# Linear attention and a highway layer on one core: the query turns of two batches moved to DMA, and batch 2's and 3's buffers rearranged

## The chip, the core and the metric

One core of a Trainium2 chip runs the whole program in one launch. The metric is the device time in microseconds, start of the program to its end. The kernel before was run 7 times: median 132.7 us, 132.04 to 135.15. One execution was taken with the hardware profiler. Its engines are TensorE (PE; PEld is its weight load), VectorE (DVE), ScalarE (ACT), GpSimd (POOL) and SyncE (SP), which issues the DMA transfers.

## What is computed

```python
# q, k, v: 8 batches, 8 heads, 576 positions, 64 columns, float32
q_s = exp(q) / sum(exp(q), over the 64 columns)
k_s = exp(k) / sum(exp(k), over the 576 positions)
kv  = einsum('bhsd,bhse->bhde', k_s, v)            # 64x64 per head
x   = einsum('bhsd,bhde->bhse', q_s, kv)           # 576x64 per head
x   = x.transpose(0, 2, 1, 3).reshape(4608, 512)   # 8 heads side by side
H   = maximum(x @ w_h, 0)                          # 512x512
T   = sigmoid(x @ w_t + b_t)
out = T * H + (1 - T) * x                          # float32
```

## The kernel before, in words

**Attention, batch by batch.** A batch's q, k and v lie in SBUF with two heads on the 128 partitions (64 positions of each), and four head pairs (c) times 9 blocks of positions (n) times 64 columns along a row. For batch b: `exp_half` (line 176) takes the exponential of half the heads of q or k on ACT, float32 in and 16 bits out (eq, ek). `q_sums` (225) sums eq over columns on DVE, `q_recip` (246) inverts the sums, and `q_scale_p` (257) multiplies eq by them on GpSimd, blocks 0 to 3 and then the rest. `cast_v` (186) turns v to 16 bits on GpSimd, with a column of ones. `kv_half` (203) accumulates ek's product with v in a two-bank PSUM tile (psk); the ones column gives k's sums, and `kv_norm` (216) divides by them on DVE into kvn.

The x matmuls need eq with its columns on the partitions. `q_trans` (261) does this turn: group 0 is blocks 0 to 3, group 1 blocks 4 to 7, group 2 block 8. For each block it issues two TensorE matmuls against the identity (`ptrans`, 67) into one PSUM bank (pq), and DVE copies the bank to qsT (line 277): 18 turns and 3 copies a batch. The bank is that of the pool ps_1, which holds one tile ("single"), unless a home is given.

`x_pair` (310), for a = 0 and 1, multiplies kvn by qsT for blocks 0 to 7 of half the heads: four matmuls of 512 columns into two banks (px), which ACT ("A") or DVE ("V") copies to xT. Block 8 is done for 64 columns at a time, inside x_pair (left=True) or by `x_left` (296), and goes to x9.

**The highway layer, chunk by chunk.** A chunk is the 512 tokens of a batch (chunks 8 and 9 hold the x9 tokens), and each has four output blocks (ob). `gate` (357) multiplies w_t by xT into a bank (pt) and ACT takes tanh in place; `carry` (368) multiplies w_h (halved and less the identity) by xT into a bank (ph), which DVE folds into dd (line 383); `blend` (388) combines pt and dd to g on DVE (line 391); `add_x` (398) adds x on GpSimd for some blocks. `out_tile` (415) turns g (and x, where it was not added) back on TensorE, copies the result to SBUF, and after every fourth block SP issues a store of 1 MB.

**PSUM.** There are eight banks: four in a ring for pt and ph (ps_ht), two held together (ps_2, `two_banks`), and one each in ps_1 (`single`) and ps_nat (`nat_bank`). A new tile in a pool waits until the tile whose place it takes has been read.

**The order of the work** is written out by hand, and each engine runs its own instructions in that order. Lines 553 to 584 give the start as a list. Everything later has a due time in slots (`at`, line 482), and the sorted slots are issued one after another. Chunk c begins at slot 8c: gate ob at 8c + 2 ob, carry one slot later, blend two slots later. Batch b's attention is placed relative to p = 8 (b - 1) (lines 516 to 549): e0, e1 for the two exponentials of q, s0, s1 for the sums, sc for the scaling, and the triples tr, kv and x for the three turns, the kv halves and the x pairs. The loads of batches 4 to 7 (line 550) are issued on SP at slot 8 (b - 3), in the same queue as the stores.

Of the kernel before, what the change touches and what calls it, by code (L numbers as in the profile page):

```python
# [9 lines left out]
FP32 = mybir.dt.float32  # L10
FP16 = mybir.dt.float16
# [7 lines left out]
def kernel(  # L19
# [10 lines left out]
    nc = tc.nc  # L30
    B, H, S, D = q.shape
    P = 128
    PAD = 128
    N9 = S // 64
# [5 lines left out]
    def heads_view(t, b):  # L40
# [9 lines left out]
    eqp = pool("eqp", 2)  # L50
    small = pool("small", 2)
    qtp = pool("qtp", 2)
    xtp = pool("xtp", 3)
    gp = pool("gp", 2)
    mo = pool("mo", 3)
    ps_ht = pool("ps_ht", 4, space=PSUM)
# [6 lines left out]
    mm = lambda o, l, r, st, sp: nc.tensor.matmul(  # L63
        o, l, r, start=st, stop=sp, skip_group_check=True
    )
# [12 lines left out]
    kvn = [consts.tile([P, 2, 2, 64], FP16, name=f"kvn{i}") for i in range(2)]  # L78
# [80 lines left out]
    def two_banks(name, dt=FP32):  # L159
        return ps_2.tile([P, 2, 2048 // (4 if dt is FP32 else 2)], dt, tag="q2", name=name)  # L160

    single = lambda name: ps_1.tile([P, 512], FP32, tag="q1", name=name)
    nat_bank = lambda name, dt=FP32: ps_nat.tile(
        [P, 512 if dt is FP32 else 1024], dt, tag="nat", name=name
# [5 lines left out]
            mm(t, ident, wide, True, True)  # L170


    ek, eq, psk, qsT = {}, {}, {}, {}
    xT, gT = {}, {}

    def exp_half(b, which, a):
# [36 lines left out]
                        n == 0, n == N9 - 1,  # L213
                    )

    def kv_norm(b):
        rz = small.tile([P, 2, 2], FP32, tag="rz", name=f"rz_{b}")
        nc.vector.reciprocal(rz, psk[b][:, :, :, 64])
        nc.vector.tensor_mul(
            kvn[b % 2], psk[b][:, :, :, 0:64], rz.broadcast_to([P, 2, 2, 64])  # L220
        )

    qsum = {}
# [37 lines left out]
    def q_trans(b, g, home=None):  # L261
# [14 lines left out]
                )  # L276
        nc.vector.tensor_copy(qsT[b][:, :, n0:n1, :], t[:, :, 0:w, :])  # L277

    def x_mm(dst, b, a, c, x, n0, n1):
        r = slice(64 * c, 64 * c + 64)  # L280
        mm(
            dst[64 * x : 64 * x + 64], kvn[b % 2][r, x, a, :],
            qsT[b][r, 2 * a + x, n0:n1, :].rearrange("p n d -> p (n d)"), True, True,
        )


    def x9_mm(t, b, c):
# [4 lines left out]
    def x9_copy(b, t, c=slice(0, 2)):  # L292
        x9v = x9.rearrange("p (a c) b d -> p c a b d", c=2)
        nc.vector.tensor_copy(x9v[:, c, :, b, :], t)

    def x_left(b):
        for c in range(2):
            name = f"px_{b}_l{c}"
            t = single(name) if c == 0 else two_banks(name)[:, 0] if b == 1 else nat_bank(name)
            t = t[:, 0:128].rearrange("p (z a w) -> p z a w", z=1, a=2)  # L300
            for a in range(2):
                for x in range(2):
                    x_mm(t[:, 0, a, :], b, a, c, x, NM, N9)
            x9_copy(b, t, slice(c, c + 1))
# [2 lines left out]

    def x_pair(b, a, how, left=False, singles=False):  # L310
        g, b2 = b // 2, b % 2
        if a == 0 and b2 == 0:
            xT[g] = xtp.tile([P, 4, NM, 2, 64], FP16, tag="xT", name=f"xT_{g}")
        if left and a == 0:
            t9 = ps_1.tile([P, 512], FP32, tag="q1", name=f"px_{b}_l")
            x9t[b] = t9[:, 0:256].rearrange("p (c a w) -> p c a w", c=2, a=2)
        if singles:
            t = [
                ps_ht.tile([P, 512], FP32, tag="ht", name=f"px_{b}_{a}_{c}")
                for c in range(2)  # L320
            ]
        else:
            t2 = two_banks(f"px_{b}_{a}")
            t = [t2[:, c] for c in range(2)]
        if left and a == 0:
            x9_mm(x9t[b], b, 0)
        for c in range(2):
            for x in range(2):
                x_mm(t[c], b, a, c, x, 0, NM)
        if left and a == 1:  # L330
            x9_mm(x9t[b], b, 1)
        dst = xT[g][:, 2 * a : 2 * a + 2, :, b2, :]
        view = lambda t: t.rearrange("p (n d) -> p n d", d=64)
        copy = {"A": nc.scalar.copy, "V": nc.vector.tensor_copy}
        if len(how) == 1:
            copy[how](dst, t2.rearrange("p c (n d) -> p c n d", d=64))  # L336
        else:
            for c in range(2):
                copy[how[c]](dst[:, c], view(t[c]))  # L339
        if left and a == 1:  # L340
            x9_copy(b, x9t[b])
# [140 lines left out]
    def at(p, *fs):  # L482
        events.setdefault(p, []).extend(fs)

    E = lambda f, *a: (lambda: f(*a))

    for c in range(1, B + 2):
        for ob in range(4):
            p = 8 * c + 2 * ob
# [6 lines left out]
    for g in range(B // 2):  # L496
        p = 16 * (g + 1)
# [6 lines left out]
    p = 8 * B + 8  # L504
# [3 lines left out]

    at(8, E(cast_v_head, 2, 0, nc.gpsimd), E(q_scale_p, 2, 0, 4), E(q_scale_p, 2, 4, 8))
    at(8.2, E(x_left, 1))  # L510
    at(9, E(exp_half, 2, "k", 0))
    at(10, E(cast_v_head, 2, 1, nc.scalar), E(exp_half, 2, "k", 1))
    at(10.5, E(blend, 0, 3))
# [7 lines left out]
    for b in range(2, B):  # L521
        p = 8 * (b - 1)
        if b > 2:
            e0, e1, s0, s1, sc = {
                3: (-2.6, -1.6, -1.1, -0.1, 1),
                4: (-5.5, -4.5, -3.7, -2.7, -2.6),
            }.get(b, (-5, -4, -3.9, -2.9, -2.8))
            at(p + e0, E(exp_half, b, "q", 0))
            at(p + e1, E(exp_half, b, "q", 1))
            at(p + s0, E(q_sums, b, 0))  # L530
            at(p + s1, E(q_sums, b, 1), E(q_recip, b))
            at(p + sc, E(q_scale_p, b, 0, 4), E(q_scale_p, b, 4, N9))
            s = p + {3: 0, 4: 0}.get(b, -0.5)
            at(s, E(exp_half, b, "k", 0), E(cast_v, b, 0))
            at(s + 0.9, E(cast_v, b, 1))
            at(s + 1, E(exp_half, b, "k", 1))
        tr, kv, x = {
# [3 lines left out]
        }.get(b, ((2, 3, 4), (4, 4), (5, 6)))  # L541
        for i in range(3):
            at(p + tr[i], E(q_trans, b, i))
        at(p + kv[0], E(kv_half, b, 0))
        at(p + kv[1], E(kv_half, b, 1), E(kv_norm, b))
        at(p + x[0], E(x_pair, b, 0, "A", b > 2))
        at(p + x[1], E(x_pair, b, 1, "AV" if b == 2 else "A", b > 2, b == 2))
        if b == 2:
            at(p + 7.6, E(x_left, 2))
    for b in range(4, B):  # L550
        at(8 * (b - 3), *[E(load, b, w) for w in "qkv"])

    for f in [
        E(warm_up, 24),
        E(exp_half, 0, "q", 0), E(q_sums, 0, 0),
        E(exp_half, 0, "q", 1), E(q_sums, 0, 1),
        E(q_recip, 0), E(q_scale_v, 0, 0, 4), E(q_scale_v, 0, 4, N9),
        E(exp_half, 0, "k", 0), E(cast_v, 0, 0),
        E(exp_half, 0, "k", 1), E(cast_v, 0, 1),
        E(q_trans, 0, 0), E(q_trans, 0, 1, lambda: two_banks("pq_0_1", FP16)[:, 0]), E(warm_up, 2), E(q_trans, 0, 2, lambda: nat_bank("pq_0_2", FP16)),  # L560
        E(warm_up, 6),
        E(kv_half, 0, 0), E(gate_bias), E(warm_up, 2), E(kv_half, 0, 1), E(kv_norm, 0),
        *[E(cast_weight, "t", k_, (nc.vector, nc.gpsimd)[k_ % 2]) for k_ in range(4)],
        E(warm_up, 4),
        E(x_pair, 0, 0, "AA"), E(warm_up, 2), E(x_pair, 0, 1, "AV", False, True), E(warm_up, 1), E(x_left, 0),
        E(exp_half, 1, "q", 0), E(q_sums_tree, 1, 0),
        E(exp_half, 1, "q", 1), E(q_sums_tree, 1, 1), E(q_recip, 1),
        *[f for k_ in range(4) for f in (E(less_one, k_), E(cast_weight, "h", k_, nc.scalar, 0.5))],
        E(q_scale_p, 1, 0, 4), E(q_scale_p, 1, 4, 8),
        E(gate, 0, 0), E(gate, 0, 1), E(gate, 0, 2, lambda: two_banks("pt_0_2")[:, 0]), E(warm_mid, 5),  # L570
        E(carry, 0, 0), E(blend, 0, 0), E(carry, 0, 1), E(exp_half, 1, "k", 0),
        E(gate, 0, 3, lambda: nat_bank("pt_0_3")), E(blend, 0, 1), E(carry, 0, 2),
        E(q_trans, 1, 0), E(blend, 0, 2), E(carry_products, 0, 3),
        E(exp_half, 1, "k", 1),
        *[E(cast_v_head, 1, c, (nc.scalar, nc.gpsimd, nc.gpsimd, nc.scalar)[c]) for c in range(4)],
        E(q_scale_p, 1, 8, N9),
        *[E(load, 2, w) for w in "qk"], E(load, 2, "v", [nc.sync, nc.sync]),
        *[E(load, 3, w) for w in "qkv"],
        E(q_trans, 1, 1), E(kv_half, 1, 0), E(kv_half, 1, 1), E(kv_norm, 1),
        E(q_trans, 1, 2), E(carry_diff, 0, 3), E(exp_half, 2, "q", 0),  # L580
        E(x_pair, 1, 0, "AV"), E(x_pair, 1, 1, "AV", False, True),
        E(q_sums_tree, 2, 0), E(exp_half, 2, "q", 1), E(q_sums_tree, 2, 1), E(q_recip, 2),
    ]:
        f()
    for p in sorted(events):
# [32 lines left out]
```

The softmax here doesn't subtract the row's maximum and nothing guards it: scores larger than these inputs give would overflow.

## Time and profile before

| | |
|---|---|
| runs | 132.7 us median of 7, 132.04 to 135.15 |
| profiled execution | 132.04 us, of which the span is 130.2 us |
| granted TensorE clock, mean | 0.988 |
| TensorE busy, span slices 69 to 114 us | 10.97 of 11, 11.96 of 12, 10.97 of 11, 10.97 of 11 us |
| TensorE idle, 36 to 57 us | 4.25 us |
| loads to landing, median | 13.7 us (q), 13.2 us (k), 13.8 us (v); 1152 KB each |
| stores of 1 MB to landing, median | 5.2 us |

The span is what the profile covers, from the first instruction to the last. A profile row gives the source line, the engine, the operation, its output and inputs by name with their shape, how often it came, the busy time and the mean duration of one, and the idle time of the engine just before such instructions with what ended it. A row of the timeline has the start and the length first, and in brackets the idle time before it and who ended that. Busy matmuls overlap: the 219 ns of a small matmul are its latency, and eight of them in a row take 0.45 to 0.6 us. In the chain of waits each row is a piece of the path that ended last, with its start and its share of that path.

### The profile page before, as it was taken

What the parts mean: (1) busy time and instruction counts of PE and PEld (TensorE: products, weight loads), DVE (VectorE), ACT (ScalarE), POOL (GpSimd) and SP (SyncE); (2) the same over time, 40 slices, a digit from 0 to 9 for tenths busy, and PEclk for the clock granted to TensorE, in tenths of its full rate; (3) what the DMA queues carried; (4) which work ended last, traced back from release to release, by engine and by line L of the source; (5) the groups of instructions that cost most, each with busy time, mean ns of one, the idle gap of its engine ahead of it and who ended that gap; (6) DMA issues with size and microseconds to landing.
All of it is one profiled execution on the core that took longest, in us unless ns stands there. A gap on an engine that the chain in (4) does not pass through costs nothing.

```text
span 130.2 us, 3470 instructions
## 1 busy us (share of the span) xinstructions
PE 114.8 (88%) x1431; PEld 64.6 (50%) x1431; DVE 99.8 (77%) x183; ACT 92.3 (71%) x129; POOL 70.3 (54%) x64
## 2 busy tenths in 40 slices
PE   4999997984988798499989999999999999999940
PEld 1345442461435346255645664465556445688930
DVE  1397537796999997986899679988997656669960
ACT  3643159987898499287979988998994666576430
POOL 2004516880299999549835990799299704600000
PEclk9999999999999999999999999999999999999995
DMA  4999999999999999996999999992034007065874
GB/s 127 371 380 388 402 401 412 411 411 413 403 413 410 402 412 412 403 411 251 290 375 413 412 267 413 405 433 118 0 146 181 0 5 322 0 252 234 362 309 140
DMA packets 15847, 40.06 MB, mean 308 GB/s; under 512 B 724, under 2 KB 1240, under 8 KB 14808
## 3 DMA queue, kind: packets, MB, share of 16 engines
q1 hardware_dynamic: 15832, 39.85, 79.3%
q8 instruction: 11, 0.18, 0.5%
q14 instruction: 4, 0.03, 0.1%
HBM read 30.41 MB, written 9.44 MB: 306 GB/s over the span
## 4 chain that ended last, share of the span: by engine, by line
PE 47%; DMA 19%; DVE 14%; POOL 8%; SPq 3%; issue 2%; ACT 2%; DVEq 0%; POOLq 0%
DMA q<-in_q_dram 19%; PE pt L63 17%; PE ph L63 15%; PE nat L63 6%; POOL eq L259 3%; PE pq L68 3%; DVE dd L383 3%; POOL g L400 3%; DVE g L391 2%; PE px L63 2%; PE psk L63 2%; SPq L95 2%; DVE r L229 2%; POOL v L192 2%; DVE xT L339 1%
## 5 line engine op out<-in xcount | busy, mean ns | idle before, releaser
L259 POOL TENSOR_TENSOR eq<-eq,r 128x1024 f16<-128x1024 f16 (+2 forms) x16 | 29.7, 1875 | 14.9 <-DVE r L247 14.3
L63 PE MATMUL pt<-xT,w16t 128*128 128x512 f16 x128 | 33.7, 379 | 2.8 <-DVE dd L383 1.3
L63 PE MATMUL ph<-xT,w16h 128*128 128x512 f16 x128 | 33.3, 380 | 1.1 <-ACT w16h L115 0.7
L365 ACT ACTIVATE pt<-pt,bt 128x512 f32<-128x512 f32 (+1 forms) x40 | 24.7, 621 | 12.0 <-PE pt L63 11.2
L391 DVE SCALAR_TENSOR_TENSOR g<-pt,dd 128x512 f16<-128x512 f32 (+1 forms) x40 | 25.0, 628 | 3.1 <-DVE dd L383 0.5
L383 DVE SCALAR_TENSOR_TENSOR dd<-xT,ph 128x512 f16<-128x512 f16 x32 | 21.8, 682 | 6.7 <-PE ph L63 6.6
L400 POOL TENSOR_TENSOR g<-g,xT 128x512 f16<-128x512 f16 x18 | 20.5, 1152 | 7.6 <-DVE g L391 7.5
L63 PEld LDWEIGHTS <-w16t 128*128 128x128 f16 x160 | 14.6, 97 | 18.1 <-issue 5.6
L180 ACT ACTIVATE eq<-q 128x1152 f16<-128x1152 f32 x16 | 18.6, 1174 | 5.2 <-DMA q<-in_q_dram 5.2
L180 ACT ACTIVATE ek<-k 128x1152 f16<-128x1152 f32 x16 | 18.6, 1172 | 1.7 <-DMA k<-in_k_dram 1.7
L63 PEld LDWEIGHTS <-w16h 128*128 128x128 f16 x160 | 13.7, 98 | 11.3 <-ACT w16h L115 2.4
L229 DVE TENSOR_REDUCE r<-eq 128x18 f32<-128x1152 f16 x12 | 16.1, 1344 | 3.8 <-ACT eq L180 3.7
L192 POOL CAST v<-v 128x1152 f16<-128x1152 f32 x12 | 13.5, 1146 | 10.0 <-DMA v<-in_v_dram 10.0
L63 PE MATMUL nat<-ident,g 128*128 128x128 f16 x142 | 17.7, 219 | 0.5 <-DVE g L391 0.2
L63 PEld LDWEIGHTS <-g 128*128 128x128 f16 x144 | 13.7, 98 | 7.1 <-DVE g L391 1.4
L336 ACT CAST xT<-px 128x1024 f16<-128x1024 f32 x11 | 11.2, 1016 | 7.2 <-PE px L63 7.2
L440 ACT COPY o<-nat 128x512 f32<-128x512 f32 x26 | 15.6, 600 | 0.1
L63 PE MATMUL warm<-wide,ident 128*128 128x512 f16 x41 | 12.8, 462 | 1.8 <-DVE wide L152 1.8
L68 PE MATMUL pq<-ident,eq 128*128 128x128 f16 x144 | 12.0, 219 | 2.7 <-DVE qsT L277 2.1
L277 DVE COPY qsT<-pq 128x1024 f16<-128x1024 f16 (+1 forms) x24 | 13.2, 553 | 1.1 <-PE pq L68 0.6
L68 PEld LDWEIGHTS <-eq 128*128 128x128 f16 x144 | 9.3, 97 | 7.0 <-issue 3.3
L63 PE MATMUL nat<-ident,xT 128*128 128x128 f16 x56 | 9.7, 219 | 0.0
(52 smaller groups left out, 100.3 us busy)
## 6 DMA issues: line engine op xcount, KB each, us to landing
out_dram<-o SPq DMA_DIRECT2D x8, 1024.0 KB, 5.2
q<-in_q_dram SPq DMA_DIRECT2D x7, 1152.0 KB, 13.7
k<-in_k_dram SPq DMA_DIRECT2D x7, 1152.0 KB, 13.2
v<-in_v_dram SPq DMA_DIRECT2D x5, 1152.0 KB, 13.8
v<-in_v_dram SPq DMA_DIRECT2D x6, 576.0 KB, 11.8
q<-in_q_dram SPq DMA_DIRECT2D x2, 576.0 KB, 4.0
k<-in_k_dram SPq DMA_DIRECT2D x2, 576.0 KB, 7.0
w32t<-in_moe_w_t_dram SPq DMA_DIRECT2D x1, 1024.0 KB, 10.9
```

Of the source, the lines that this page charges most:

```text
L63: mm = lambda o, l, r, st, sp: nc.tensor.matmul(o, l, r, start=st, stop=sp, skip_group_check=True)
L68: nc.tensor.matmul(o, i, ident, is_transpose=True, start=True, stop=True, skip_group_check=True,)
L180: nc.scalar.activation(dst[b][:, :, 2 * a : 2 * a + 2, :], in32[which][b][:, 2 * a : 2 * a + 2].rearrange("p c n d -> p n c d"), AF.Exp,)
L192: (eng or nc.gpsimd).tensor_copy(o, i)
L229: nc.vector.reduce_sum(qsum[b][:, :, h], eq[b][:, :, h, :], axis=AX.X)
L259: nc.gpsimd.tensor_mul(e, e, r.broadcast_to(list(e.shape)))
L277: nc.vector.tensor_copy(qsT[b][:, :, n0:n1, :], t[:, :, 0:w, :])
L365: nc.scalar.activation(ps, ps, AF.Tanh, bias=bt2[:, ob : ob + 1], scale=0.5)
L383: nc.vector.scalar_tensor_tensor(dd, xv(ob), -0.5, ps, op0=ALU.mult, op1=ALU.max)
L391: nc.vector.scalar_tensor_tensor(gv(ob), th, 1.0, dd, op0=ALU.add, op1=ALU.mult)
L400: nc.gpsimd.tensor_add(gv(ob), gv(ob), xv(ob))
L440: nc.scalar.copy(o, flat(t))
```

## The change

Four things are rearranged, and the values computed stay the same.

1. Batches 6 and 7: `q_trans` is replaced by `q_turn`, which issues two transposing DMA transfers on SP (blocks 0 to 3, then 4 to 8) from eq to a tile qsD in SBUF; the x matmuls read it with a stride. The exponentials, sums and scaling of these batches come one slot earlier. The transfers are due at slot p - 2.05.
2. Batch 2: kv_norm is done for each half (a) by itself, the x pairs come earlier and use ps_nat and ps_1 as their banks, both pairs' copies go half by half (ACT and ACT, then ACT and DVE), and its `x_left` comes later.
3. Batch 1: the x pairs use banks of the ring (the last half one of the two-bank tile), and their copies come ahead of batch 2's first exponential.
4. Batches 2 and 3: the last turn (block 8) uses the two-bank tile instead of the single bank. The sums and the scaling of batch 4, and the sums of batch 5, come later.

```diff
+    ht_bank = lambda name: ps_ht.tile([P, 512], FP32, tag="ht", name=name)
+    one_of_two = lambda name: two_banks(name)[:, 0]
...
-    def kv_norm(b):
-        rz = small.tile([P, 2, 2], FP32, tag="rz", name=f"rz_{b}")
-        nc.vector.reciprocal(rz, psk[b][:, :, :, 64])
+    def kv_norm(b, a0=0, a1=2):
+        w = a1 - a0
+        rz = small.tile([P, 2, w], FP32, tag=f"rz{w}", name=f"rz_{b}_{a0}")
+        nc.vector.reciprocal(rz, psk[b][:, :, a0:a1, 64])
         nc.vector.tensor_mul(
-            kvn[b % 2], psk[b][:, :, :, 0:64], rz.broadcast_to([P, 2, 2, 64])
+            kvn[b % 2][:, :, a0:a1], psk[b][:, :, a0:a1, 0:64],
+            rz.broadcast_to([P, 2, w, 64]),
         )
...
+    turned = (6, 7)
+
+    def q_turn(b, n0, n1):
+        if n0 == 0:
+            qsD[b] = qtp.tile([P, 2 * N9, P], FP16, tag="qsT", name=f"qsD_{b}")
+            qsT[b] = qsD[b].rearrange("p (n a) (x k) -> p (a x) n k", a=2, x=2)
+        nc.sync.dma_start_transpose(
+            out=qsD[b][:, 2 * n0 : 2 * n1, :],
+            in_=eq[b][:, n0:n1].rearrange("p n c d -> p (n c d)"),
+        )
+
     def x_mm(dst, b, a, c, x, n0, n1):
         r = slice(64 * c, 64 * c + 64)
-        mm(
-            dst[64 * x : 64 * x + 64], kvn[b % 2][r, x, a, :],
-            qsT[b][r, 2 * a + x, n0:n1, :].rearrange("p n d -> p (n d)"), True, True,
-        )
+        rhs = qsT[b][r, 2 * a + x, n0:n1, :]
+        if b not in turned:
+            rhs = rhs.rearrange("p n d -> p (n d)")
+        elif n1 - n0 == 1:
+            rhs = rhs[:, 0]
+        else:
+            dst = dst.rearrange("p (n d) -> p n d", d=64)
+        mm(dst[64 * x : 64 * x + 64], kvn[b % 2][r, x, a, :], rhs, True, True)
...
-            t = single(name) if c == 0 else two_banks(name)[:, 0] if b == 1 else nat_bank(name)
+            t = single(name) if c == 0 else one_of_two(name) if b > 0 else nat_bank(name)
...
-    def x_pair(b, a, how, left=False, singles=False):
+    def x_pair(b, a, how, left=False, homes=None):
...
-        if singles:
-            t = [
-                ps_ht.tile([P, 512], FP32, tag="ht", name=f"px_{b}_{a}_{c}")
-                for c in range(2)
-            ]
+        if homes:
+            t = [home(f"px_{b}_{a}_{c}") for c, home in enumerate(homes)]
...
+    at(16.2, E(x_left, 2))
...
-                4: (-5.5, -4.5, -3.7, -2.7, -2.6),
+                4: (-5.5, -4.5, -2.8, -1.5, -1.4),
+                5: (-5, -4, -3.4, -2.7, -2.6),
+                6: (-6, -5, -4.9, -3.9, -3.8),
+                7: (-6, -5, -4.9, -3.9, -3.8),
             }.get(b, (-5, -4, -3.9, -2.9, -2.8))
...
-            2: ((5, 6, 6.9), (4, 6.2), (7, 7.5)),
-            3: ((3.5, 4.9, 5.1), (4, 4), (5.9, 6.9)),
+            2: ((5, 6, 7.1), (4, 6.2), (6.5, 7.2)),
+            3: ((3.5, 4.9, 4.95), (4, 4), (5.9, 6.9)),
             4: ((2, 3, 4), (4.5, 4.5), (5.9, 6.9)),
         }.get(b, ((2, 3, 4), (4, 4), (5, 6)))
-        for i in range(3):
-            at(p + tr[i], E(q_trans, b, i))
+        if b in turned:
+            at(p - 2.05, E(q_turn, b, 0, 4), E(q_turn, b, 4, N9))
+        else:
+            for i in range(3):
+                home = (lambda: two_banks("pq_t", FP16)[:, 0]) if b < 4 and i == 2 else None
+                at(p + tr[i], E(q_trans, b, i, home))
         at(p + kv[0], E(kv_half, b, 0))
-        at(p + kv[1], E(kv_half, b, 1), E(kv_norm, b))
-        at(p + x[0], E(x_pair, b, 0, "A", b > 2))
-        at(p + x[1], E(x_pair, b, 1, "AV" if b == 2 else "A", b > 2, b == 2))
         if b == 2:
-            at(p + 7.6, E(x_left, 2))
+            at(p + kv[0], E(kv_norm, b, 0, 1))
+            at(p + kv[1], E(kv_half, b, 1), E(kv_norm, b, 1, 2))
+        else:
+            at(p + kv[1], E(kv_half, b, 1), E(kv_norm, b))
+        homes = (nat_bank, single) if b == 2 else None
+        at(p + x[0], E(x_pair, b, 0, "AA" if b == 2 else "A", b > 2, homes))
+        at(p + x[1], E(x_pair, b, 1, "AV" if b == 2 else "A", b > 2, homes))
...
-        E(q_trans, 1, 2), E(carry_diff, 0, 3), E(exp_half, 2, "q", 0),
-        E(x_pair, 1, 0, "AV"), E(x_pair, 1, 1, "AV", False, True),
-        E(q_sums_tree, 2, 0), E(exp_half, 2, "q", 1), E(q_sums_tree, 2, 1), E(q_recip, 2),
+        E(q_trans, 1, 2), E(carry_diff, 0, 3),
+        E(x_pair, 1, 0, "AV", False, (ht_bank, ht_bank)),
+        E(x_pair, 1, 1, "AV", False, (ht_bank, one_of_two)),
+        E(exp_half, 2, "q", 0), E(q_sums_tree, 2, 0), E(exp_half, 2, "q", 1),
+        E(q_sums_tree, 2, 1), E(q_recip, 2),
```

More of the change, by code (lines that the diff above doesn't have):

```diff
@@ L170, in warm_mid @@
             mm(t, ident, wide, True, True)
-    ek, eq, psk, qsT = {}, {}, {}, {}
+    ek, eq, psk, qsT, qsD = {}, {}, {}, {}, {}
     xT, gT = {}, {}
@@ L564 @@
         E(warm_up, 4),
-        E(x_pair, 0, 0, "AA"), E(warm_up, 2), E(x_pair, 0, 1, "AV", False, True), E(warm_up, 1), E(x_left, 0),
+        E(x_pair, 0, 0, "AA"), E(warm_up, 2), E(x_pair, 0, 1, "AV", False, (ht_bank, ht_bank)), E(warm_up, 1), E(x_left, 0),
         E(exp_half, 1, "q", 0), E(q_sums_tree, 1, 0),
```

## The prediction

> **What bounds the kernel now.** I read the page's first row and its groups, then a table of the span cut into stages, then the chain of waits in order of time, and last the timeline around the two places that the change touches. The page's rows say who is busy and what one query turn costs:
>
> ```profile
> PE 114.8 (88%) x1431; PEld 64.6 (50%) x1431; DVE 99.8 (77%) x183; ACT 92.3 (71%) x129; POOL 70.3 (54%) x64
> L68 PE MATMUL pq<-ident,eq 128*128 128x128 f16 x144 | 12.0, 219 | 2.7 <-DVE qsT L277 2.1
> L277 DVE COPY qsT<-pq 128x1024 f16<-128x1024 f16 (+1 forms) x24 | 13.2, 553 | 1.1 <-PE pq L68 0.6
> ```
>
> A share over the whole span hides the stages. The stage table (busy us of each engine, number of instructions, granted clock, DMA share, GB/s) separates them:
>
> ```profile
> 36.00:57.00 21.00, 16.75 (x268) 9.19 (x266) 19.54 (x35) 15.39 (x21) 17.90 (x14) 1.00 1.04 408
> 57.00:69.00 12.00, 11.45 (x166) 6.49 (x163) 10.05 (x17) 10.63 (x15) 8.64 (x6) 1.00 0.91 326
> 80.00:92.00 12.00, 11.96 (x173) 6.92 (x173) 11.01 (x19) 11.23 (x16) 8.59 (x6) 1.00 0.77 307
> 92.00:103.00 11.00, 10.97 (x162) 6.29 (x156) 9.61 (x17) 8.11 (x13) 8.59 (x6) 1.00 0.23 97
> ```
>
> From 69 to 114 us TensorE has no gap: what leaves its queue there leaves the span, and what stalls it there lengthens the span. From 36 to 57 us it idles 4.25 us and VectorE is 93% busy. The chain of waits (start, us, what) names who holds that stage, and gives the price of the turns where TensorE is the bound:
>
> ```profile
> 37.81 1.89 POOL eq L259
> ...
> 40.88 3.78 POOL g L400 x4
> ...
> 47.53 1.91 POOL eq L259
> 49.44 0.05 issue
> 49.48 0.62 PE pq L68 x8
> ...
> 96.67 0.45 PE pq L68 x8
> ...
> 97.98 0.53 PE pq L68 x8
> ...
> 99.71 0.11 PE pq L68 x2
> ```
>
> GpSimd carries the chain from batch 2's query scaling to 49.44 us. A batch's 18 turns cost TensorE 0.45 + 0.53 + 0.11 = 1.09 us on the chain; the 219 ns of the group row are pipelined latencies. Then two stalls, in the timeline:
>
> ```profile
> 52.63 1.34 DVE L229 TENSOR_REDUCE r<-eq 128x18 f32<-128x1152 f16 x1
> 53.89 0.68 DVE L277 COPY qsT<-pq 128x1024 f16<-128x1024 f16 x1
> 54.62 0.27 PE L68 MATMUL pq<-ident,eq 128*128 128x128 f16 x2 [1.20 <-DVE qsT L277]
> 55.42 0.22 PE L63 MATMUL px_l<-qsT,kvn 64*64 64x64 f16 x2 [0.52 <-DVE qsT L277]
> ```
>
> Batch 4's query sum stands ahead of batch 3's evacuation, and the last turn waits for the one bank it shares. A third stall of 0.52 us (px_l at 67.35, waiting for kvn) has the same form: batch 5's sum (65.41) stands ahead of batch 4's kv norm.
>
> **The change, part by part.** All sums are against the profiled execution: 132.04 us, a span of 130.2 us and 1.84 us around it. The median of the runs is 132.7; I subtract the same microseconds from it.
>
> *Batch 1's x copies ahead of batch 2's exponentials.* ACT now begins batch 2's first exponential at 30.03, when its load lands, and the first xT copy only at 31.10. In the new order two copies of 0.5 us come first (px is there at about 30.4), the exponentials end at about 33.8 instead of 33.2, and DVE, which then has its xT copies behind it by 32.1 instead of 32.99, runs the second tree sum from 33.9 instead of 34.10. The reciprocal that opens GpSimd's scaling (35.94) comes some 0.3 us sooner; bounds: 0.4 gained to 0.4 lost, if the exponentials come later than that. I take -0.3.
>
> *Batch 2 by pairs.* One more reciprocal and multiply on DVE: together 0.60 us undivided (0.18, 0.42). Halved they cost nothing extra, all fixed they cost 0.6; the nearest row, the 128x128 copy of x9 (two in 0.42), says about 0.15 extra. ACT copies 2 x 0.59 instead of 1.01, another 0.2. The second pair's matmuls now wait for ACT to empty two banks used twice, and queued behind them is the gate of chunk 2. But DVE's copy of the last quarter comes after a sum and a dd as before, near 45 us. All this lies beside GpSimd's gapless row of work to 51.7 us, which the change leaves in order: I take 0; without that cover it would cost up to 0.4. The earlier first pair ends in a longer wait at 49.4 and gains nothing.
>
> *Last turns in their own bank, sums of batch 4 later.* DVE from 52.08, by the chain's durations: rz and kvn to 52.71, the two qsT copies to 53.6, so px can start at 53.8 instead of 55.42: 1.6 us. New wait: this turn needs the two banks that hold psk, so it waits for kvn (52.71), with ph of chunk 2 queued behind it, 0.3 us, inside those 53.8. But the sums are not gone, they are late next: dd 54.2, sum 55.45, g 56.05, sum 57.3, reciprocal 57.7, x9 58.05, dd 58.65, g 59.25. The second gate of chunk 3 needs that g's bank: 59.3 instead of 60.65. So -1.3; bounds -0.4 and -1.7 (all three TensorE gaps here). GpSimd's scaling of batch 4 moves from 57.20 to 57.9 and ends at 62.1; TensorE wants its second half near 62 (63.24 less 1.3): level. Batch 5's sums go behind the kv norm: the 0.52 us stall goes, -0.5 (bounds 0, -0.5). Sum up to 69 us: -2.1.
>
> *Turns of batches 6 and 7 by DMA.* Removed: 36 turns and 6 evacuations. TensorE gains 2 x 1.09 = 2.2 us, all on its gapless stretch. DVE's 2 x 1.65 us (0.68 + 0.68 + 0.29) had slack: 0. The x matmuls now read runs of 64 elements out of a stride; pt reads xT in such runs at 379 ns for 512 columns, px its unbroken rows at 400: 0. The exponentials come one slot earlier, ending at 77.2 instead of 78.9 for batch 6, and push a tanh by 0.5 us whose blend comes only two slots later: 0 (ACT has 0.8 us of idle in 80 to 92; if it binds, +0.3).
>
> Added: on SP's queue two transfers per batch, 256 and 320 KB. SP waits for the scaling before each; behind them in its queue is one output store, ready at 84.44 and then some 1.5 us late, for which nobody waits (three output buffers). Nothing in this trace transposes by DMA. The cost has two terms.
>
> First the queue. These rows are one microsecond each:
>
> ```profile
> 86.00:87.00 1.00, 1.00 (x12) 0.62 (x10) 0.83 (x2) 1.00 (x3) 1.00 (x2) 1.00 1.16 476
> 87.00:88.00 1.00, 1.00 (x10) 0.53 (x8) 1.00 (x3) 0.60 (x1) 1.00 (x2) 1.00 1.00 423
> 88.00:89.00 1.00, 1.00 (x81) 0.90 (x78) 0.80 (x2) 0.94 (x2) 1.00 (x2) 1.00 0.71 295
> 89.00:90.00 1.00, 1.00 (x26) 0.38 (x12) 0.72 (x3) 1.00 (x2) 1.00 (x2) 1.00 0.14 41
> ```
>
> The last thing in them is the 1.05 MB store issued at 84.44; counted back from the end (41 + 295 + 423 KB, then 0.29 MB at 476), batch 7's loads drain at 86.4. They are issued at 73.47 to 76.44, ahead of the transposes (scaling ends near 82.2 and 84.5), in one queue, so batch 6's transposes start to move only after them. These loads stand in line since 61 us, where the gain so far is 1.6 us: 84.8 after the change.
>
> Second the rate, where two rules of the Trainium skill disagree. A 128x128 16-bit turn costs 0.06 us of the chain here (1.09/18). "VectorE: DVE Perf Modes", section "The three transpose paths", puts one such turn at 1309 ns by DMA and advises TensorE: a rule against this change. Its 18 blocks would be an estimated 23.6 us per batch. "DMA: Bandwidth & Descriptors", section "Latency and other measured facts", gives a transposing DMA 261 GB/s for strided data, 0.126 us per 32 KB block, an estimated 2.26 us per batch (0.59 MB). The nearest row here is a plain transfer, at 406 to 412 GB/s in the full windows. The single-turn price must hold a fixed part that many blocks in one transfer share, so I take 261 GB/s and keep both ends. For the landing: the 128 KB store took 2.9 us, of which 0.3 is transfer, so 2.6 fixed; behind a backlog its front is hidden, between 0 and 2.6, I take 1.5.
>
> Batch 6: 84.8 + 2.26 + 1.5 = 88.6. TensorE wants it at 90.08 - 2.1 - 1.09 = 86.9. New stall 1.7 us, every later matmul behind it. Batch 7: the sums move ahead by 1.9 us, the scaling ends at 95.9 instead of 97.8 (times of the profile before); wanted at 101.43 - 1.1 = 100.3. On an empty queue (0 GB/s from 90 to 96) the second transfer takes 2.6 + 0.328/0.261 = 3.9 us of the 4.4 there are: no stall.
>
> Sum: -0.3 - 1.3 - 0.5 - 2.2 + 1.7 = -2.6 us; 132.7 - 2.6 = 130.1 (129.4 in the profiled execution).
>
> **Rivals.** *Hidden.* The transposes overtake or land in time: no stall, -4.3, 128.4. For it: the DMA share is 0.14 and then 0 after 89 us. Against it: loads show 13 us to landing where 1.15 MB at 410 GB/s is 2.9, so the queue is in order and deep. *Level.* At r GB/s batch 6 stalls 590/r - 0.6 and batch 7 328/r - 1.8 (us, with r in KB per us); both together eat 4.3 us at r = 137, or 0.24 us per block. From 125 to 152 GB/s the time is within 0.5% (about what a measurement of this kernel can tell from no change): 132.7. *Slower.* The one mechanism: the DMA's rate per 128x128 block, at TensorE's wait for batch 6's x matmuls; it decides from 0.24 us per block. At 0.41 us, midway (as a ratio) between 0.126 and 1.309, r is 80: stalls 6.8 and 2.3, -4.3: +4.8, 137.5. At 1.309 us it is over 30 us slower. For it: the rule for a single turn, and no row of this trace shows the transfer; against it: the two transfers carry 8 and 10 blocks each.
>
> **How the numbers follow.** Likeliest, as summed: 0.40, own range 129.2 to 131.5 (terms of batch 3 and the landing at their bounds). Hidden: 0.18. Level: 0.12. Slower: 0.30. Faster 0.58, same 0.12, slower 0.30. The range goes from 128.2 to 136.0: below is only 0.03, above is the worse half of the slower case.
>
> **What would show it.** Right: no wait of pq for qsT near 53; px of batch 3 about 1.6 us earlier but the following gates 1.3; TensorE idle 1 to 3 us before batch 6's px, released by a DMA, and none before batch 7's; transposes landing 2 to 4 us after the loads drain. Wrong: a wait before batch 7's px as well (rate under 180 GB/s), transposes that land before the loads do, or a wait of GpSimd's scaling of batch 3 for its sums.

## The result and the profile after

| | before | changed |
|---|---|---|
| median | 132.72 us (64 runs) | 131.77 us (27 runs, 130.81 to 133.92) |
| profiled execution | 132.04 us, span 130.2 us | 131.22 us, span 129.4 us |
| TensorE busy, 80 to 92 us | 11.96 of 12 us | 9.74 of 12 us |

The ratio of the times is 0.9935 [0.9913, 0.9957]: 0.86 us faster, where 2.6 us were forecast. Executions over 1.5% above the fastest of their kernel are left out of the ratios, not of the medians; the profiles of m2_adds_first_sums_behind, m4_m2_store_late and m5_m3_turn4_late are of slower executions, so of m2 a second profile is read, and of the other two only single rows and differences up to batch 6's x matmuls.

First the page's row of engines and the two groups of the query turn:

```profile
PE 113.2 (87%) x1395; PEld 62.5 (48%) x1395; DVE 97.5 (75%) x179; ACT 92.2 (71%) x130; POOL 69.9 (54%) x64
L69 PE MATMUL pq<-ident,eq 128*128 128x128 f16 x104 | 8.5, 219 | 2.6 <-POOL eq L264 1.1
L282 DVE COPY qsT<-pq 128x1024 f16<-128x1024 f16 (+1 forms) x16 | 9.3, 585 | 1.2 <-PE pq L69 0.7
```

The 36 turns of batches 6 and 7 are gone (four more of the missing 40 now write pq_t). The groups' releasers tell the story ahead: the turns wait for GpSimd's scaling (eq) where they waited for the evacuation (qsT).

The stages, same columns as in the prediction:

```profile
36.00:57.00 21.00, 19.23 (x282) 10.07 (x282) 19.38 (x34) 16.71 (x22) 17.13 (x14) 1.00 1.04 408
57.00:69.00 12.00, 11.16 (x163) 6.23 (x162) 10.47 (x19) 10.73 (x15) 8.71 (x7) 1.00 1.03 391
...
80.00:92.00 12.00, 9.74 (x142) 5.27 (x140) 9.25 (x15) 9.72 (x13) 9.13 (x7) 1.00 0.96 288
92.00:103.00 11.00, 10.97 (x155) 5.86 (x150) 6.97 (x12) 9.19 (x15) 9.28 (x8) 1.00 0.52 150
```

TensorE's idle time from 36 to 57 us fell from 4.25 to 1.77 us. But the stage from 80 to 92 us, gapless before, now has 2.26 us without TensorE. TensorE's own timeline names its waits (start, length, in brackets the wait and who ended it):

```profile
52.01 0.29 PE L69 MATMUL pq_t<-ident,eq 128*128 128x128 f16 x2 [0.21 <-DVE kvn L223]
53.09 0.22 PE L64 MATMUL px_l<-qsT,kvn 64*64 64x64 f16 x2
...
61.83 0.62 PE L69 MATMUL pq<-ident,eq 128*128 128x128 f16 x8 [0.81 <-POOL eq L264]
65.38 0.22 PE L64 MATMUL px_l<-qsT,kvn 64*64 64x64 f16 x2
...
77.27 0.22 PE L64 MATMUL px_l<-qsT,kvn 64*64 64x64 f16 x2 [0.44 <-DVE kvn L223]
...
86.58 0.48 PE L64 MATMUL psk<-v,ek 64*64 64x65 f16 x36 [0.24 <-POOL v L195]
90.01 0.22 PE L64 MATMUL px_l<-qsD,kvn 64*64 64x64 f16 x2 [1.98 <-DMA qsD<-eq]
...
100.28 0.22 PE L64 MATMUL px_l<-qsD,kvn 64*64 64x64 f16 x2
```

The 1.20 and 0.52 us waits at batch 3 and the 0.52 us wait at batch 4's px_l are gone. Five have come: 0.21 us for the kv norm at batch 3's last turn, 0.81 us for GpSimd at batch 4's second turn, 0.44 us for the kv norm at batch 5, 0.24 us for v's cast and 1.98 us for the transposes at batch 6.

The chain of waits (start, us, what) moves from GpSimd to VectorE, back to GpSimd, and then to a DMA:

```profile
46.76 1.91 POOL eq L264
...
55.74 1.27 DVE r L234
...
57.59 4.20 POOL eq L264 x2
...
83.27 6.70 DMA qsD<-eq
```

It now follows the whole scaling of batch 4 (4.20 us), and the second of batch 6's transposes from its issue to its landing.

A profile's start-up differs from run to run: batch 1's first q exponential starts anywhere from 17.98 to 20.07 us, when its load lands. I therefore compare distances between the first px_l rows of successive batches, one cycle of the attention each:

| us from px of the batch before to px of | batch 4 | batch 5 | batch 6 | batch 7 |
|---|---|---|---|---|
| before | 11.93 | 11.38 | 11.35 | 11.35 |
| changed | 12.29 | 11.89 | 12.74 | 10.27 |
| m6_batch3_alone | 12.30 | 11.38 | 11.35 | 11.34 |
| r1_tensor_67 | 12.31 | 11.37 | 11.35 | 11.35 |
| r2_dma_alone | 11.93 | 11.90 | 11.45 | 11.27 |
| r4_dma_7 | 12.30 | 11.38 | 11.88 | 11.27 |
| r3_sums_behind | 12.29 | 11.38 | 11.81 | 12.38 |
| r5_v7_late | 12.30 | 11.89 | 11.46 | 11.27 |
| m1_adds_first | 12.31 | 11.89 | 12.76 | 10.27 |
| m2_again | 12.30 | 11.37 | 12.94 | 10.27 |
| m3_m2_v7_late | 12.30 | 11.38 | 10.72 | 10.71 |

Only batch 7's cycle is what the prediction counted on: 11.35 - 1.09 = 10.26. What the first three batches gave can be anchored too: from GpSimd's first scaling of batch 3 to batch 3's px it is 7.89 us before (47.53 to 55.42) and 6.33 us after (46.76 to 53.09).

### The profile page after: what moved, and what is told of

The parts are those of the page before. It is cut to its first block, busy times and chain, and to the rows that moved or that the text cites. A ratio compares the mean times of both kernels' runs of the same rounds, so it can differ in the third digit from the quotient of the medians.

```text
span 129.4 us, 3405 instructions
## 1 busy us (share of the span) xinstructions
PE 113.2 (87%) x1395; PEld 62.5 (48%) x1395; DVE 97.5 (75%) x179; ACT 92.2 (71%) x130; POOL 69.9 (54%) x64
## 4 chain that ended last, share of the span: by engine, by line
PE 36%; DVE 25%; DMA 16%; POOL 7%; issue 6%; ACT 4%; SPq 3%; DVEq 0%; POOLq 0%
PE pt L64 12%; PE ph L64 12%; DMA q<-in_q_dram 11%; POOL eq L264 7%; DVE dd L401 6%; DVE g L409 6%; DMA qsD<-eq 5%; PE nat L64 5%; DVE r L234 3%; PE px L64 2%; PE pq L69 2%; PE psk L64 2%; SPq L96 2%; DVE qsT L282 2%; ACT eq L183 2%
## 5 line engine op out<-in xcount | busy, mean ns | idle before, releaser
L418 POOL TENSOR_TENSOR g<-g,xT 128x512 f16<-128x512 f16 x18 | 20.5, 1152 | 7.7 <-DVE g L409 7.7
L354 ACT CAST xT<-px 128x1024 f16<-128x1024 f32 x10 | 10.2, 1016 | 6.6 <-PE px L64 6.6
L69 PE MATMUL pq<-ident,eq 128*128 128x128 f16 x104 | 8.5, 219 | 2.6 <-POOL eq L264 1.1
L282 DVE COPY qsT<-pq 128x1024 f16<-128x1024 f16 (+1 forms) x16 | 9.3, 585 | 1.2 <-PE pq L69 0.7
L69 PEld LDWEIGHTS <-eq 128*128 128x128 f16 x108 | 6.7, 97 | 6.8 <-POOL eq L264 2.8
L357 ACT CAST xT<-px 128x512 f16<-128x512 f32 x8 | 4.3, 590 | 7.8 <-PE px L64 7.8
```

Source lines behind the costliest of these rows:

```text
L69: nc.tensor.matmul(o, i, ident, is_transpose=True, start=True, stop=True, skip_group_check=True,)
L418: nc.gpsimd.tensor_add(gv(ob), gv(ob), xv(ob))
```

## The experiments

The theory after the two traces: batches 1 to 5 rearranged bring the 2.0 us by which batch 4's px came earlier (67.35 to 65.38, the start-up's differences included), and the DMA part gives about half of it back, because its relief of 1.09 us a batch is spent on new waits (transposes behind the loads, the query sum ahead of the kv norm). That GpSimd's scaling ahead of add_x is a third was seen after the first four runs. The rivals: one of these waits alone is to blame, so that taking it away gives the forecast's time; or the rearrangement is what fell short. Medians are given beside ratios to the kernel before, timed on the same chip. Line numbers of rows are those of each kernel.

**r1_tensor_67**: the changed kernel with batches 6 and 7 turned by TensorE, at the old slots.

```diff
-    turned = (6, 7)
+    turned = ()
-                6: (-6, -5, -4.9, -3.9, -3.8),
-                7: (-6, -5, -4.9, -3.9, -3.8),
```

> The changed kernel with batches 6 and 7 turned by TensorE again, at the slots of before; the rearrangement of batches 1 to 5 is kept. Theory (the rearrangement is worth the 2.0 us that px of batch 4 came earlier, and the DMA part gives 1.1 us of it back): 130.7 us, ratio to before 0.985, faster than the changed kernel. Rival (the gain of the rearrangement is caught up later by another engine whatever turns the queries): 131.7 to 132.5 us, ratio 0.993 to 1.0.

Measured: 130.99 us, 0.9903 [0.987, 0.9935]. That is nearer to the theory than to its rival. Its cycles of batches 5 to 7 are those of the kernel before, and so it is the rearrangement alone: -1.29 us where the prediction has -2.1. It is faster than the whole change, by 0.42 us by the two ratios (0.78 us by the medians). The two intervals overlap a little, so this run by itself does not show that the DMA part costs time; the next one does.

**r2_dma_alone**: the other part by itself, on the kernel before.

```diff
+                6: (-6, -5, -4.9, -3.9, -3.8),
+                7: (-6, -5, -4.9, -3.9, -3.8),
...
+        if b in turned:
+            at(p - 2.05, E(q_turn, b, 0, 4), E(q_turn, b, 4, N9))
```

> The kernel before with the DMA turns of batches 6 and 7 and their earlier exponentials, sums and scaling, and nothing else of the change. Theory: TensorE is relieved of 2.2 us, but waits for batch 5's kv norm (0.4) and for the transposes (some 2) and loses a little more; no gain or a loss, 132.7 to 133.4 us. TensorE waits for qsD once, before batch 6's px, 1.3 to 2 us. Rival (the DMA turns carry the gain): 131.0 to 131.8 us.

Measured: 133.58 us, 1.0091 [1.0057, 1.0124], slower. TensorE's waits from 68 to 110 us (engine, tile and line, who ended them: total, times, longest):

```profile
PE px_l L63 <- DVE kvn L219: 1.7, 3, 0.7
PE nat L63 <- POOL g L415: 0.8, 1, 0.8
PE psk L63 <- POOL v L192: 0.3, 1, 0.3
```

The time is just above the expected range, and the wait for the transposes that was expected did not come: the DMA part loses with waits for VectorE and GpSimd only. Of the 1.7 us 0.5 is batch 4's wait, which the kernel before has too; the other 1.2 and the 1.1 from GpSimd use up the relief of 2.2. The cycles of batches 5 to 7 add up to 34.62 us, against 34.08 before; the excess of 0.54 us lies in no wait of this list. A stall takes more than its listed idle time: batch 7's cycle is 11.27 us, 1.01 above the 10.26 that the relief alone would give, and the only wait listed in it is the 0.83 us for g.

**r3_sums_behind**: the changed kernel with the first sum of batches 6 and 7 behind the previous batch's kv norm.

```diff
-                6: (-6, -5, -4.9, -3.9, -3.8),
-                7: (-6, -5, -4.9, -3.9, -3.8),
+                6: (-6, -5, -3.95, -3.9, -3.8),
+                7: (-6, -5, -3.95, -3.9, -3.8),
```

> The changed kernel with the first query sum of batches 6 and 7 moved behind the kv norm of batch 5 and 6 (s0 from -4.9 to -3.95); all other slots stay. Theory (the landing of batch 6's transposes is the last thing at its px, whatever the kv norm does): px of batch 5 about 0.5 us earlier, the wait for the transposes longer by as much, the time that of the changed kernel within 0.3 us (131.8). Rival (the kv norm behind the sums is what costs): 0.5 to 1.1 us less than the changed kernel, 130.7 to 131.3.

Measured: 132.75 us, 1.0018 [0.9984, 1.0051]: both expectations missed, it is a microsecond slower than the changed kernel. TensorE's waits from 68 to 110 us:

```profile
PE nat L64 <- POOL g L418: 1.8, 1, 1.8
PE psk L64 <- POOL v L195: 1.1, 2, 0.6
```

The waits for kvn went, but the scaling, which needs the sums, starts later on GpSimd, and the additions and casts behind it come later still. So there is a second moved step, which neither expectation had priced.

**r4_dma_7**: only batch 7 by DMA, where the queue is empty.

```diff
-    turned = (6, 7)
+    turned = (7,)
-                6: (-6, -5, -4.9, -3.9, -3.8),
```

> The changed kernel with only batch 7 turned by DMA; batch 6 turned by TensorE at the slots of before. Theory (batch 7's transposes find an empty queue and cost nothing, batch 6's are the loss): 0.5 to 1.1 us below the kernel with both on TensorE, 129.6 to 130.2 us, no wait of TensorE for qsD. Rival (a DMA turn costs as much as it saves wherever it is put): the time of the kernel with both on TensorE, 130.7.

Measured: 131.32 us, 0.9933 [0.99, 0.9967], not better than r1_tensor_67; the theory missed. Batch 7's transposes delay nobody, but TensorE waits 0.47 us for kvn at batch 6 and 0.82 us for GpSimd's g: 1.29 us against a relief of 1.09. The relief is used up without any wait for a transpose.

**r5_v7_late**: the changed kernel with batch 7's v loaded after batch 6's transposes.

```diff
-        at(8 * (b - 3), *[E(load, b, w) for w in "qkv"])
+        at(8 * (b - 3), *[E(load, b, w) for w in ("qkv" if b < 7 else "qk")])
+    at(38, E(load, 7, "v"))
```

> The changed kernel with batch 7's load of v issued after batch 6's transposes instead of ahead of them; nothing else. Theory (behind the wait for the transposes stand two waits made by the earlier slots: the kv norm behind the query sum, 0.7 us, and out_tile's turn behind an add that GpSimd now does after the scaling, 0.8 to 1.8 us): the transposes land 3 us sooner, the wait for qsD goes, px of batch 6 waits for kvn, the wait for GpSimd's g appears, and the time stays within 0.6 us of the changed kernel, 131.2 to 132.4. Rival (the queue of loads ahead of the transposes is the whole loss): 1.3 to 2 us less, 129.8 to 130.5.

Measured: 131.73 us, 0.9949 [0.9917, 0.9981]: no gain, although the transposes now land 3.4 to 3.5 us after their issue (6.4 before) and nobody waits for them. TensorE's timeline shows what was under that wait:

```profile
89.52 0.22 PE L64 MATMUL px_l<-qsD,kvn 64*64 64x64 f16 x2 [0.69 <-DVE kvn L223]
96.67 0.23 PE L64 MATMUL nat<-ident,g 128*128 128x128 f16 x1 [0.83 <-POOL g L418]
```

The 1.98 us wait for the DMA covered these two; without it they stand in the open.

**m1_adds_first**: the changed kernel with GpSimd's scaling of batches 6 and 7 behind add_x of output block 1, as it is for the other batches.

```diff
-                6: (-6, -5, -4.9, -3.9, -3.8),
-                7: (-6, -5, -4.9, -3.9, -3.8),
+                6: (-6, -5, -4.9, -3.9, -3.45),
+                7: (-6, -5, -4.9, -3.9, -3.45),
```

> The changed kernel with the scaling of batches 6 and 7 due at p - 3.45 instead of p - 3.8, so that GpSimd does the add of output block 1 before it, as the kernel before did; the transposes' slots stay. Theory: GpSimd was idle before its scaling, so the add costs it nothing; the waits for v's cast (0.24) and for g go, those for kvn and for the transposes of batch 6 stay: 131.2 to 131.8 us, no more than 0.5 below the changed kernel. Rival (the scaling and with it the transposes come a whole add later): 132.3 to 133.

Measured: 131.05 us, 0.9874 [0.9826, 0.9922]. The wait for v's cast is gone, that for the transposes is 2.42 us, and the cycles are those of the changed kernel. The median is just below the expected range, and the profile does not show where its 0.7 us come from; the interval overlaps that of the changed kernel.

**m2_adds_first_sums_behind**: both, (-6, -5, -3.95, -3.9, -3.45).

> The same with the first query sum of batches 6 and 7 behind the kv norms as well (s0 = -3.95). Theory: no wait for kvn at px of batch 5, none for GpSimd; the transposes of batch 6, behind the loads, are the one wait left, 1 to 3 us; px of batch 7 10.3 us after that of batch 6. 129.6 to 131.2 us. Rival (the sums behind the norm make the scaling late, as the slower run with this edit alone may be read): 132 us or more, and a wait for the transposes before batch 7's px.

Measured: 131.61 us, 0.9903 [0.9861, 0.9946], just above the expected range. A second profile:

> The kernel with the adds first and the sums behind the kv norms once more, for a profile beside the store's: a wait for the transposes of 1.5 to 2.5 us before batch 6's px, no other wait of TensorE over 0.3 us from there on, px of batch 7 10.3 to 10.8 us after that of batch 6.

It took 131.80 us. Batch 5's cycle is 11.37 again, and batch 6 has one long wait left (beside 0.19 us for dd):

```profile
90.69 0.22 PE L64 MATMUL px_l<-qsD,kvn 64*64 64x64 f16 x2 [2.17 <-DMA qsD<-eq]
```

**m3_m2_v7_late**: m2 together with r5's late load of v.

> The same with batch 7's v loaded after batch 6's transposes. Theory: all four waits are gone, and what is left is the 2.2 us that TensorE is relieved of, against the kernel with both batches on TensorE (131.0): 128.6 to 129.4 us, ratio to before 0.970 to 0.976; at most 0.5 us of waiting for batch 7's transposes. Rival (turns by DMA give nothing back on this kernel because another engine is as full as TensorE there): 130.5 to 131.2.

Measured: 129.8 us, 0.9783 [0.9735, 0.9831], the best version, 1.2 us ahead of r1_tensor_67 and about the time that was forecast for the change, though above the expected 128.6 to 129.4 us. TensorE's only listed wait from 68 to 110 us, and SP's issues:

```profile
PE pt L64 <- DVE dd L401: 0.4, 2, 0.2
```

```profile
81.36 3.63 SPq L291 DMA_TRANSPOSE qsD<-eq  x2
85.04 0.71 SPq L96 DMA_DIRECT2D v<-in_v_dram  x1
```

The three repairs pay together. None of them alone (r3, m1, r5) nor the two of m2 comes to this time; the best of those by its ratio is m1, 0.9874. The cycles are 10.72 and 10.71, 0.45 above 10.26. 0.19 us is the wait for dd. The rest is in the kv matmuls, which take 1.07 us against 0.78 in r1. Their rows in r1 and in m3, and GpSimd's and the weight load's (PEld) in m3:

```profile
86.52 0.78 PE L64 MATMUL psk<-v,ek 64*64 64x65 f16 x72
...
83.56 2.24 POOL L195 CAST v<-v 128x1152 f16<-128x1152 f32 x2
85.27 1.07 PE L64 MATMUL psk<-v,ek 64*64 64x65 f16 x72
85.86 0.36 PEld L64 LDWEIGHTS <-ek 64*64 64x64 f16 x35 [0.21 <-issue]
```

In m3 the weight loads stop half way and go on at 85.86, 0.06 us after the second half of v is cast (83.56 + 2.24 = 85.80); at batch 7 it is 96.57 after 96.52. The cast still stands behind the scaling on GpSimd, so a short form of that wait is left. It is read from the trace; no run takes it away.

**m4_m2_store_late**: m2 with the store that stands behind batch 6's transposes issued after those of batch 7 (slot 46.05).

> The kernel with the adds first and the sums behind the kv norms, with one store of 1 MB (the first half of token group 1) issued after batch 6's x pairs instead of right behind its second transpose; batch 7's loads stay ahead of the transposes. Rival (the store behind them in the queue takes the DMA engines from the second transpose, which landed just when that store's bytes ended): the second transpose lands about 2 us after SP is done with it instead of 3.5, the wait before batch 6's px is 1 us or less, 130.2 to 130.8 us. Theory (the loads ahead are what delays it, SP's issue of the second transpose itself takes 2.4 to 3.1 us there instead of 1.3): the landing moves by less than 0.5 us, the time stays at 131.2 to 131.8.

Measured: 132.17 us, 0.9923 [0.9877, 0.997], above both expected ranges. Batch 6 waits as long as in m2:

```profile
90.61 0.22 PE L64 MATMUL px_l<-qsD,kvn 64*64 64x64 f16 x2 [2.46 <-DMA qsD<-eq]
```

The store, which moves bytes at the same time, is not the cause; the wait goes when the last load ahead is moved (m3).

**m5_m3_turn4_late**: m3 with batch 4's second and third turn later, since TensorE waits 0.81 us for that second turn.

```diff
-            4: ((2, 3, 4), (4.5, 4.5), (5.9, 6.9)),
+            4: ((2, 4.1, 4.55), (4.5, 4.5), (5.9, 6.9)),
```

> The version with adds first, sums behind and v of batch 7 late, with batch 4's second turn put behind the next gate and out_tile (slot 28.1 instead of 27) and its last turn behind its kv half. Theory (the later sums of batch 4 made its scaling late, and TensorE stands 0.8 us at that turn with work behind it that needs nothing of it): the wait of pq for GpSimd's eq goes and px of batch 4 comes 12.3 - 0.7 = 11.6 us after that of batch 3; 129.0 to 129.3 us against 129.8. Rival (the wait only moves to the next thing, the kv norm or dd on DVE): 11.9 us or more between the two px, 129.6 to 130.0.

Measured: 129.83 us, 0.9778 [0.9734, 0.9822], no gain on m3. The rival was right that the wait only moves, though not where to:

```profile
64.92 0.48 PE L64 MATMUL psk<-v,ek 64*64 64x65 f16 x36 [0.25 <-POOL v L195]
66.01 0.48 PE L64 MATMUL psk<-v,ek 64*64 64x65 f16 x36 [0.61 <-POOL v L195]
```

Instead of 0.81 us for the scaling, TensorE waits 0.25 + 0.61 us for v's cast, which stands behind that scaling on GpSimd.

**m6_batch3_alone**: on the kernel before, only the last turn of batch 3 in the two-bank tile, the later sums and scaling of batch 4 and the later sums of batch 5.

```diff
-                4: (-5.5, -4.5, -3.7, -2.7, -2.6),
+                4: (-5.5, -4.5, -2.8, -1.5, -1.4),
+                5: (-5, -4, -3.4, -2.7, -2.6),
...
-            3: ((3.5, 4.9, 5.1), (4, 4), (5.9, 6.9)),
+            3: ((3.5, 4.9, 4.95), (4, 4), (5.9, 6.9)),
```

> The kernel before with only the edits of batches 3 to 5: batch 3's last turn in the two-bank tile, the sums and scaling of batch 4 later, the sums of batch 5 later; batches 1, 2, 6 and 7 as before. Theory (this is most of what the rearrangement is worth, and 0.8 us of it is lost at batch 4's scaling): px of batch 3 1.4 to 1.7 us earlier against the start of batch 1's exponentials, px of batch 4 1.0 to 1.4 us; 131.3 to 131.7 us, ratio 0.991 to 0.994. Rival (batch 1's order, not this, starts GpSimd's row of work sooner and is the larger part): 132.0 to 132.5.

Measured: 131.32 us, 0.9912 [0.9879, 0.9944]: -1.17 us, nearly all that r1_tensor_67 has. Scaling of batch 3 to px of batch 3 is 6.33 us, as in the changed kernel, so the edits of batches 1 and 2 are not needed for it.

## Why the prediction was wrong

The sign was right, and the mechanisms that it named were at work; the sum was too large by 1.7 us. The rearrangement brought 1.3 us where 2.1 were forecast, and the DMA part lost about 0.4 (r1 against the whole change) where 0.5 were to be gained. Three steps failed. The slots of batches 6 and 7 were moved ahead at a cost of 0, weighed on ACT alone; on VectorE and GpSimd they make TensorE wait. Batch 4's scaling was called level with TensorE's need; TensorE waits 0.81 us for it. And batch 6's transposes were to land 3.8 us after the loads; they took 5.2.

**Batch 1's copies, forecast -0.3; batch 2 by pairs, forecast 0.** From batch 1's first q exponential to batch 2's scaling it is 16.99 us before and 16.81 after, but 16.95 in r1, which has the same edit, and 17.00 in m6, which has not: 0 to 0.2. From batch 2's scaling to batch 3's it is 11.59 before and 11.60 after: the 0 held.

**Batch 3's last turn, forecast 1.6 at px.** Measured 1.56 (7.89 to 6.33). The new wait for the psk banks, 0.3 forecast, was 0.21.

**Batches 4 and 5 up to px, forecast -1.3 - 0.5.** Measured -1.2 together (m6 -1.17; 1.56 less the 0.36 by which batch 4's cycle grew). The 0.52 us wait for kvn did go. The step that failed here is "GpSimd's scaling of batch 4 moves from 57.20 to 57.9 and ends at 62.1; TensorE wants its second half near 62 ...: level". VectorE's timeline in the changed kernel:

```profile
53.20 0.69 DVE L401 SCALAR_TENSOR_TENSOR dd<-xT,ph 128x512 f16<-128x512 f16 x1 [0.45 <-PE ph L64]
53.80 1.34 DVE L234 TENSOR_REDUCE r<-eq 128x18 f32<-128x1152 f16 x1
...
55.66 1.34 DVE L234 TENSOR_REDUCE r<-eq 128x18 f32<-128x1152 f16 x1
...
74.53 1.34 DVE L234 TENSOR_REDUCE r<-eq 128x18 f32<-128x1152 f16 x1
...
76.80 0.42 DVE L223 TENSOR_TENSOR kvn<-psk,rz 128x256 f16<-128x256 f32 x1
```

Taken from px of batch 3, the forecast had the scaling start at +4.1 us (57.9 - 53.8), end at +8.3 and be wanted at +8.2. It starts at +4.5 (57.59 - 53.09), since dd waits 0.45 us for ph ahead of the sums, ends at +8.7, and TensorE is there at +7.9 (61.83 - 0.81). Two errors of 0.3 to 0.4 us in what was called level make the 0.81 us wait. m5 says what is late there: GpSimd's later work too, not that turn alone.

**Exponentials, sums and scaling of batches 6 and 7 one slot earlier, forecast 0.** This was priced on ACT only, and it was wrong on two other queues. On VectorE, the last two rows above: batch 6's sum (74.53) stands ahead of batch 5's kv norm (76.80), and TensorE waits 0.44 us for that norm. It is the very form of stall that the prediction saw batch 5's sums lose. At batch 6 it is 0.69 us, as r5 shows. On GpSimd, the timelines of the kernel before and of the changed one:

```profile
76.06 2.35 POOL L400 TENSOR_TENSOR g<-g,xT 128x512 f16<-128x512 f16 x2
82.23 4.19 POOL L259 TENSOR_TENSOR eq<-eq,r 128x1024 f16<-128x1024 f16 x2 [3.82 <-DVE r L247]
```

```profile
75.21 1.15 POOL L418 TENSOR_TENSOR g<-g,xT 128x512 f16<-128x512 f16 x1
79.06 4.19 POOL L264 TENSOR_TENSOR eq<-eq,r 128x1024 f16<-128x1024 f16 x2 [2.69 <-DVE r L252]
83.20 1.15 POOL L418 TENSOR_TENSOR g<-g,xT 128x512 f16<-128x512 f16 x1
84.30 2.23 POOL L195 CAST v<-v 128x1152 f16<-128x1152 f32 x2
```

Before, both additions of the chunk ran ahead of the scaling. Now the scaling (slot 36.2) has passed the second one (36.5), which with v's cast stands behind its 4.19 us. The prediction did not speak of this move. TensorE waits 0.83 us for g and 0.26 us for v where nothing covers it (r5). m3, which undoes both orders and moves the load, is 1.97 us faster than the changed kernel: 0.51 us at batch 5, and 23.01 - 21.43 = 1.58 us at batches 6 and 7.

**The relief of TensorE, forecast 2.2.** Right: 11.35 to 10.27 us at batch 7.

**The wait for batch 6's transposes, forecast 1.7.** Measured 1.98; that it is so near is luck, by terms that were wrong both ways. The rows of one microsecond and SP's issues:

```profile
84.00:85.00 1.00, 1.00 (x6) 0.41 (x5) 0.42 (x2) 1.00 (x4) 1.00 (x2) 1.00 2.26 271
85.00:86.00 1.00, 1.00 (x25) 0.66 (x27) 0.46 (x1) 1.00 (x3) 1.00 (x2) 1.00 0.34 32
```

```profile
80.98 5.38 SPq L291 DMA_TRANSPOSE qsD<-eq  x2
86.46 0.54 SPq L461 DMA_DIRECT2D out_dram<-o  x1
92.44 3.63 SPq L291 DMA_TRANSPOSE qsD<-eq  x2
```

The loads drain at about 84.8, as forecast (271 of 410 KB, and 32). The transposes' landing, forecast 3.8 us later (88.6), was 5.2 us later (90.0), outside the 2 to 4 us named as a sign of being right. Two terms were too small. The front was not hidden behind the backlog: SP is still issuing the second transpose when the loads have drained, until 86.36 (80.98 + 5.38), and the DMA moves next to nothing meanwhile (the 32 KB). And the transfer of 18 blocks, 2.26 us in the forecast, is an estimated 2.7 to 3.1 us at the 0.15 to 0.17 us per block that the empty queue showed (last section). No run separates the two, and why SP takes so long there stays open. TensorE, too, came later, at 88.03 and not at 86.9, held up by the waits at batches 4, 5 and 6 that the sum did not have. The late landing thus covered waits that the forecast did not know, which is why taking it away alone gave nothing (r5, 0.9949). Nor does undoing the two orders alone help much: m2, which keeps the landing, has 0.9903, just what r1 has without any DMA turn. Either mistake is enough to lose the gain; with both mended it is 0.9783 (m3).

**Batch 7's transposes, forecast no wait, 3.9 us for the second transfer.** Right: no wait, and 3.4 us.

The likeliest case had the right mechanisms but one. The rivals did not happen: the transposes were not hidden, and their rate, the one mechanism of the slower case, was not what cost. What all the cases lacked was the order of the queues that the earlier slots pass.

## What to carry to other kernels

When a step is moved in a hand-written order, list on every in-order engine what it now passes, and price the wait of whoever needs that: here a 1.34 us sum moved ahead of a 0.42 us norm and a 4.19 us scaling ahead of a 1.15 us addition cost more than the 2.2 us of matmuls that were saved. A wait that covers others is not worth its length; take them all away in one kernel before judging a part (129.8 us with three repairs, 131.05 to 132.75 with any one). Two terms called level can be a stall of the size of their joint error, here 0.8 us.

## What the runs showed of the hardware

A DMA transpose held the issuing queue longer behind loads than on an empty queue. SP takes 1.24 and 1.34 us for batch 7's 256 and 320 KB on an empty queue, and 1.85 and 3.09 us for batch 6's behind the loads. A plain load of 1152 KB takes it 0.43 us (q), and 1.0 to 1.1 us for k and v right behind it. From issue to landing a transpose takes 3.1 and 3.4 us on the empty queue, and 6.4 and 6.7 us behind the loads. With the last 1152 KB load moved behind them (m3), batch 6's two land in 3.2 and 3.4 us.

Of the two rules that the prediction weighed, the single-turn price of 1309 ns ("VectorE: DVE Perf Modes", section "The three transpose paths", in the Trainium skill) does not multiply by the number of blocks: eight landed 3.1 us after issue, ten 3.4 us, which is 0.15 us for each of the two more. While batch 7's first transpose moves alone, the DMA carries 188 KB in a microsecond:

```profile
94.00:95.00 1.00, 1.00 (x10) 0.62 (x9) 0.68 (x1) 1.00 (x2) 1.00 (x2) 1.00 1.00 188
```

That is an estimated 0.17 us per 32 KB block (32.8/188). Both are somewhat above the estimated 0.126 us per block that the prediction took from the other rule, and below the 0.24 us from which the change would have lost by its rate.
